# A fused attention and mixture-of-experts kernel: half-row score products on unpadded keys, and another order of gathers and weight splits in the first block of the last layer

## The chip, the cores and the metric

One Trainium2 chip, one of its cores. The metric is the device time of one execution in microseconds (us). The kernel before has a median of 1069.2 us over three runs (1066.33 to 1070.52). All data are float32 in the reference.

## What is computed

Three layers, one after the other, on 2304 tokens (4 sequences of 576) of width 512.

```python
# 1: attention with decay, 8 heads of 64
scores = scale * np.matmul(q, k.transpose(0, 1, 3, 2))
Dmat = np.where(rel >= 0, gamma[:, None, None] ** rel[None, :, :], 0.0)
attn = np.matmul(scores * Dmat[None], v)
# 2: 8 experts, the two best of each token by noisy logits
h = np.maximum(x[mask] @ w1[e], 0.0)                  # 512 -> 1024
out[mask] += top2_w[mask, k, None] * (h @ w2[e])      # 1024 -> 512
# 3: one dense layer of width 2048
h = x @ w_in
g = h * np.cos(h)
return g @ w_out
```

## The kernel before

**Layout of the time.** The program is written for one core with a manual order: each engine runs its instructions in the order in which the Python code emits them. Four stages follow one another in the span: attention with gating and routing (0 to about 165 us), expert 0's second part and experts 1 to 7 (to 639 us), the first block of the last layer (to 689 us), and eight more blocks of the last layer.

**Attention.** There are 20 tiles, five a sequence: four of 128 tokens (`c < 4`) and a tail of 64 (`c == 4`). The loop over `j` runs from -2 to 20. In iteration `j` it issues the loads of tile `j + 4` on SyncE's queue (SP: `load_tile`, L329 queries, L335 keys, L343 keys and values by rows), scales the queries of tile `j + 2` (`decay`, L419, on GpSimd from tile 4 on), makes the score products of tile `j + 1` (`scores`), the gate products of `j - 1` (`gate`, L501) and the outputs of `j` (`outputs`: L469 state, L474 scores times values, L488 the new state), and stores the rows of `j - 1` (L514, SP again). Eight heads lie as four pairs `hp`: partitions 0 to 63 hold one head of a pair, 64 to 127 the other (`s`).

The keys of a full tile lie in a tile `kb` with zeros beside them: for half `s`, only the 64 partitions of that half hold keys, the others hold zeros that were set once at the start (L318, L319). So each score product (L445) runs over all 128 rows although half of them are zeros:

```python
kb[64 s : 64 s + 64, hp, s, :] = keys          # two loads of 512-byte pieces a tile, L335
matmul(p[:, i, s, :], KT[j][:, hp, s, :], QT[j][:, hp, :])    # L445, 8 a tile, 2 passes each
```

The product is masked by VectorE from PSUM (L446), two instructions of 128x512 a tile. PSUM tiles named `ph` come from three buffers. The tail tile has its own form (L455).

**The planner.** Routing (top-2, ranks, tables) is a generator of VectorE instructions that `pump()` puts between the attention's own. `spent(pe, dve)` adds planned TensorE and VectorE time; `pump` emits routing steps as long as the planned VectorE time is less than the planned TensorE time plus a slack. The scores count 0.87 us of TensorE a half. After the attention, the first half of expert 0 (`layer1(0, 0)`, `layer2(0, 0)`) is TensorE work beside the last routing steps.

**Zeros.** `ZERO` gives, for each of seven stores of 1 MB of zeros to the end of `ys` (`zero_overflow`, L373, SP's queue), the iteration at which it is issued; 20 and more count steps behind the attention loop.

**Last layer.** A block is two tiles of 128 tokens; there are nine. `mlp1(i, parts)` makes eight products (L1192, 24 matmuls of 128x256 each), and for each of them `h cos h`: ScalarE L1197 and L1203, VectorE L1198, L1199, L1200, L1204; then the result is split in a high part (ScalarE, L1209) and a low part `gl` (L1210). `mlp2` multiplies by the second weights (L1222, 96 matmuls of 128x512). The rows of block `i + 1` are fetched by `fetch` (L1152, 16 indirect gathers on GpSimd) and combined and transposed by `turn2` (ScalarE L1170 and L747, VectorE L1171, L755 and L748), which writes `x2h` and `x2l`, the operands of `mlp1(i + 1)`.

In block 0 eight weight units are still to be split into high (ScalarE, L289) and low part (L290) by `split_unit`. `SP0` gives the steps of `mlp1` after which one is split, `SPP` those of them whose low part is GpSimd's (0, 3, 6, 9, of which three are used); the others are VectorE's. `FS0 = 1` gather is emitted a step of block 0, the rest behind `mlp1`. `GLP0 = 4`: `gl` of the first four products is GpSimd's in block 0, that of the last four VectorE's; in later blocks all are GpSimd's (`GLP = 8`).

Of the kernel before, what the change touches and what calls it, by code (L numbers as in the profile page):

```python
# [10 lines left out]
F32 = mybir.dt.float32  # L11
# [14 lines left out]
NC = 5  # L26
# [19 lines left out]
ZERO = (11, 13, 22, 27, 27, 29, 33)  # L46
# [3 lines left out]
GLP = 8  # L50
GLP0 = 4
FS = 1
FS0 = 1
SPP = (0, 3, 6, 9)
SP0 = (0, 1, 2, 3, 4, 5, 6, 7, 8, 9)
# [159 lines left out]
def moe_kernel(ctx, tc, x, out, dbg=None, phases="ABC"):  # L215
# [99 lines left out]
    for i in range(LOOK):  # L315
        t = ca.tile([128, HP, 2, 128], F32, name=f"kb{i}")
        eng = nc.gpsimd if i else nc.vector
        eng.memset(t[:64, :, 1, :], 0.0)  # L318
        eng.memset(t[64:, :, 0, :], 0.0)  # L319
        KB.append(t)  # L320
# [10 lines left out]
    def load_k(j):  # L331
        b, c = divmod(j, NC)
        kb, src = (KB[(4 * b + c) % LOOK], x["kt"][4 * b + c]) if c < 4 else (KBT, x["ktt"][b])
        for s in range(2):
            nc.sync.dma_start(kb[s * 64:(s + 1) * 64, :, s, :],  # L335
                              src[s * 64:(s + 1) * 64].rearrange("p (a t) -> p a t", a=HP))
        KT[j] = kb
# [98 lines left out]
    def scores(j):  # L436
        b, c = divmod(j, NC)
        am = wk.tile([128, HP, 2, 128], F32, name="am", bufs=2)
        if c < 4:
            for h2 in range(2):  # L440
                p = ps.tile([128, 2, 2, 128], F32, name="ph", bufs=PHB)
                for i in range(2):
                    hp = 2 * h2 + i
                    for s in range(2):
                        nc.tensor.matmul(p[:, i, s, :], KT[j][:, hp, s, :], QT[j][:, hp, :], start=True, stop=True)  # L445
                nc.vector.tensor_tensor(  # L446
                    am[:, 2 * h2:2 * h2 + 2].rearrange("p a s q -> p (a s) q"),
                    p.rearrange("p a s q -> p (a s) q"),
                    bs["mask"][:, None, :].to_broadcast([128, 4, 128]), op=OP.mult)
                AM[j] = am  # L450
                yield
# [445 lines left out]
    for j in range(-2, NTILE + 1):  # L897
# [12 lines left out]
        if 0 <= j + 1 < NTILE:  # L910
            decay_v(j + 1)
            for _ in scores(j + 1):
                spent(0.87, 0.6)
                pump()
# [261 lines left out]
    def mlp1(i, parts):  # L1176
# [7 lines left out]
        for s in range(10):  # L1184
# [20 lines left out]
            if 0 <= s - 2 < 8:  # L1205
# [4 lines left out]
                (nc.gpsimd if g < (GLP if i else GLP0) else nc.vector).tensor_tensor(  # L1210
# [91 lines left out]
    for i in range(len(blocks)):  # L1302
# [3 lines left out]
        for _ in mlp1(i, parts):  # L1306
            if n in SP0 and state["split"] < len(units):
                split_unit(nc.gpsimd if n in SPP else nc.vector)
            steps(fg, FS if i else FS0)
            n += 1  # L1310
        while state["split"] < len(units):
            split_unit()
        drain(fg)
        drain(turn2(i + 1))
# [23 lines left out]
```

## Time and profile before

| | us |
|---|---|
| median of three runs | 1069.2 (1066.33 to 1070.52) |
| profiled execution | 1059.2 |
| its span, first to last instruction | 1057.3 |
| TensorE busy, mean granted clock | 995.3, 0.966 |
| VectorE, GpSimd, ScalarE busy | 688.6, 445.8, 370.1 |

TensorE's share is 94%, so what counts is where TensorE is not busy, and where it is busy with more or slower work than needed. The share is an average over stages that differ: in the attention the DMA engines are nearly as full as TensorE, in the last layer they are nearly idle.

### The profile page before, as it was taken

The page shows a single profiled execution, that of the slowest core. Times are in us where ns is not written, and L with a number is a line of the kernel's source. Part 1 is how long each engine was busy: PE and PEld are TensorE (multiplying, and loading weights), DVE is VectorE, ACT ScalarE, POOL GpSimd, SP SyncE. Part 2 cuts the span into 40 slices and gives each one's busy share as a digit, 9 for nine tenths or more (in the row PEclk, how much of TensorE's full clock was granted, in tenths as well). Part 3 has the DMA queues.
Part 4 walks back from the last instruction along what each step waited for, and adds up shares of the span by engine and source line. Part 5 has one row for each costly group of instructions (what it writes and reads, how often), then busy time and mean ns, then how long its engine had stood idle before and what let it go on. Part 6 is the DMA issues. An engine that isn't in the chain of part 4 may idle for free.

```text
span 1057.3 us, 17808 instructions
## 1 busy us (share of the span) xinstructions
PE 995.3 (94%) x6845; PEld 928.5 (88%) x6845; DVE 688.6 (65%) x1364; ACT 370.1 (35%) x657; POOL 445.8 (42%) x439
## 2 busy tenths in 40 slices
PE   8989986879899999999899989999999999999998
PEld 7778875869898989989899989798988989899897
DVE  4688971638587676858586447865848567484662
ACT  2422410323141323323142334543535445353451
POOL 6343436351506142341500064736547474564711
PEclk9999988869999999999999999989999999999999
DMA  9898494336576565657563544211010110101110
GB/s 277 270 261 266 120 295 121 100 101 182 157 209 185 180 204 164 215 147 238 160 209 102 141 138 135 73 33 48 21 46 23 43 35 32 50 18 46 30 24 20
DMA packets 85846, 135.37 MB, mean 128 GB/s; under 512 B 13376, under 2 KB 51648, under 8 KB 85760
## 3 DMA queue, kind: packets, MB, share of 16 engines
q1 hardware_dynamic: 76048, 113.74, 36.2%
q0 software_dynamic: 9568, 20.20, 7.3%
q8 instruction: 55, 0.90, 0.4%
q10 hardware_dynamic: 144, 0.27, 0.1%
q14 instruction: 31, 0.25, 0.1%
HBM read 106.25 MB, written 35.26 MB: 134 GB/s over the span
## 4 chain that ended last, share of the span: by engine, by line
PE 84%; DMA 5%; issue 4%; DVE 4%; SPq 1%; ACT 1%; POOL 0%; ACTq 0%; DVEq 0%; POOLq 0%
PE py L1222 18%; PE ph L818 14%; PE ph L797 10%; PE ph L1192 9%; PE pt L797 8%; PE pt L1192 5%; DMA qr<-qt 4%; PE ptab L797 4%; PE ptab L818 3%; PE pt L818 3%; PE ptab L1192 3%; PE ph L445 1%; PE py L818 1%; PE py L469 1%; PE py L474 1%
## 5 line engine op out<-in xcount | busy, mean ns | idle before, releaser
L722 POOL DMA_INDIRECT rows<-xs,gidx x140 | 139.1, 993 | 227.9 <-DVE xt L755 186.7
L1152 POOL DMA_INDIRECT y<-ys,slot x144 | 139.9, 972 | 56.3 <-issue 26.5
L1210 POOL TENSOR_TENSOR gl<-t,gh 128x512 fp32r<-128x512 f32 x68 | 88.6, 1303 | 140.8 <-issue 111.1
L818 PE MATMUL ph<-hh,hb 128*128 128x360 f32 (+2 forms) x312 | 98.8, 317 | 4.9 <-issue 4.6
L818 PE MATMUL ph<-hh,lb 128*128 128x360 f32 (+2 forms) x312 | 98.9, 317 | 4.2 <-issue 4.1
L818 PE MATMUL ph<-hl,hb 128*128 128x360 f32 (+2 forms) x312 | 98.9, 317 | 2.5 <-issue 2.5
L1200 DVE TENSOR_SCALAR t<-t 128x512 int32<-128x512 int32 x72 | 72.8, 1011 | 2.5
L1171 DVE SCALAR_TENSOR_TENSOR y<-y,wts,y 128x128 f32<-128x128 f32 x72 | 34.4, 510 | 59.1 <-DMA y<-ys,slot 52.1
L1198 DVE TENSOR_SCALAR t<-t 128x512 f32<-128x512 f32 x72 | 37.4, 519 | 51.0 <-ACT t L1197 51.0
L747 ACT ACTIVATE xh<-xt 128x512 fp32r<-128x512 f32 (+1 forms) x35 | 21.6, 617 | 137.7 <-DVE xt L755 118.7
L818 PEld LDWEIGHTS ph<-hh,lb 128*128 128x128 f32 x312 | 60.9, 195 | 6.8 <-issue 6.7
L818 PEld LDWEIGHTS ph<-hh,hb 128*128 128x128 f32 x312 | 61.4, 197 | 5.1 <-issue 5.1
L818 PEld LDWEIGHTS ph<-hl,hb 128*128 128x128 f32 x312 | 60.8, 195 | 4.3 <-issue 4.3
L1203 ACT ACTIVATE t<-t,cbias 128x512 f32<-128x512 f32 x72 | 51.9, 722 | 32.9 <-DVE t L1200 32.1
L802 ACT ACTIVATE hh<-pt 128x256 fp32r<-128x256 f32 (+2 forms) x48 | 20.0, 416 | 110.0 <-PE pt L797 77.2
L1222 PE MATMUL py<-hd,gl 128*128 128x512 f32 (+1 forms) x152 | 57.7, 380 | 0.8 <-DVE gl L1210 0.8
L1222 PE MATMUL py<-hb,gl 128*128 128x512 f32 (+1 forms) x152 | 58.4, 384 | 0.0
L1222 PE MATMUL py<-lb,gh 128*128 128x512 f32 (+1 forms) x152 | 58.4, 384 | 0.0
L1222 PE MATMUL py<-hb,gh 128*128 128x512 f32 (+1 forms) x152 | 58.3, 384 | 0.0
L290 POOL TENSOR_TENSOR lb<-st,hb 128x1024 fp32r<-128x1024 f32 x7 | 16.9, 2423 | 97.4 <-PE ptab L797 58.1
L797 PE MATMUL ph<-xh,ha 128*128 128x360 f32 (+3 forms) x236 | 47.7, 321 | 10.5 <-issue 6.1
L797 PE MATMUL ph<-xl,ha 128*128 128x360 f32 (+3 forms) x236 | 49.0, 322 | 9.2 <-issue 9.0
(307 smaller groups left out, 2747.2 us busy)
## 6 DMA issues: line engine op xcount, KB each, us to landing
st<-w SPq DMA_DIRECT2D x64, 512.0 KB
kv<-kv SPq DMA_DIRECT2D x16, 512.0 KB
ci<-wi SPq DMA_DIRECT2D x16, 512.0 KB
wc<-cy SPq DMA_DIRECT2D x32, 256.0 KB
ci<-wo SPq DMA_DIRECT2D x16, 512.0 KB
st<-wc SPq DMA_DIRECT2D x16, 512.0 KB
ys<-c_zero SPq DMA_DIRECT2D x7, 1024.0 KB
qr<-qt SPq DMA_DIRECT2D x20, 256.0 KB
```

The lines of the kernel that those rows point to most:

```text
L722: nc.gpsimd.indirect_dma_start(out=t[:, g, :], out_offset=None, in_=xs.rearrange("n (a d) -> (n a) d", a=4), in_offset=bass.IndirectOffset ...
L747: nc.scalar.activation(hi, src, AF.Copy)
L797: nc.tensor.matmul(p[:, :n], w[a][:, dc, (f % 2) * 128:(f % 2 + 1) * 128], XE[e, g][b][:, dc, :n], start=(i == 0), stop=(i == 3 * DC - 1))
L818: nc.tensor.matmul(p[:, :n], w[a][:, f % 2, c * 128:(c + 1) * 128], HE[e, g][b][:, f, :n], start=(i == 0), stop=(i == 3 * FC - 1))
L1152: nc.gpsimd.indirect_dma_start(out=t[:, g, :], out_offset=None, in_=(ys if i else ys[:FIRST]).rearrange("n (a d) -> (n a) d", a=4), in_off ...
L1171: nc.vector.scalar_tensor_tensor(y0[:, g], y1[:, g], w1, y0[:, g], op0=OP.mult, op1=OP.add)
L1192: nc.tensor.matmul(p[:, f, :], w[a][:, dc, f * 128:(f + 1) * 128], X2[i][b][:, dc, :], start=(k == 0), stop=(k == 3 * DC - 1))
L1198: nc.vector.tensor_scalar(t, t, -MAGIC, None, op0=OP.add)
L1200: nc.vector.tensor_scalar(t.bitcast(I32), t.bitcast(I32), 0x7FFFFFFF, None, op0=OP.bitwise_and)
L1203: nc.scalar.activation(t, t, AF.Sin, scale=-1.0, bias=cbias[:, 1:2])
L1210: (nc.gpsimd if g < (GLP if i else GLP0) else nc.vector).tensor_tensor(fl(gl), T[g], fl(gh.bitcast(F32)), op=OP.subtract)
L1222: nc.tensor.matmul(ps_[tb][:, :c1 - c0], parts[f // 2][b][:, f % 2, tb * 128:(tb + 1) * 128], w[a][:, f % 2, c0:c1], start=(f + k == 0), s ...
```

## The change

In the attention, the zeros beside the keys go. `kb` holds 128 partitions of keys, loaded by one transfer of 2 KB pieces, and each score product runs over the 64 rows of its half, the products of the two halves taking turns and writing two PSUM tiles. The planner counts 0.5 us a half in place of 0.87. Two of the seven zero stores, issued at iterations 11 and 13, move to steps 18 and 24 behind the attention loop.

In block 0 of the last layer, the gathers of block 1 are emitted four a step, so all 16 in the first four steps. No split is GpSimd's in the loop of `mlp1`: six are VectorE's (after steps 0, 1, 3, 5, 7, 9), the last two are GpSimd's behind the loop, each followed by one step of `turn2(1)`. `gl` is VectorE's for products 0 to 4 and GpSimd's for 5 to 7.

```diff
 PHB = 3
 STB = 3
 QPOOL = 4
-ZERO = (11, 13, 22, 27, 27, 29, 33)
+ZERO = (22, 27, 27, 29, 33, 38, 44)
 LOOK = 4
 WJ = 3
 T0_AT = ()
-GLP = 8
-GLP0 = 4
 FS = 1
-FS0 = 1
-SPP = (0, 3, 6, 9)
-SP0 = (0, 1, 2, 3, 4, 5, 6, 7, 8, 9)
+FS0 = 4
+SP0 = (0, 1, 3, 5, 7, 9)
 
 CG_1 = (6, 8, 9, 11, 13, 15)
 CG_2 = (1, 2, 3, 4, 5)
@@
     dq = [dq0[:, :HP * 128]] + [ca.tile([128, HP * 128], F32, name=f"dq{c}") for c in range(1, NC)]
     KB = []
     for i in range(LOOK):
-        t = ca.tile([128, HP, 2, 128], F32, name=f"kb{i}")
-        eng = nc.gpsimd if i else nc.vector
-        eng.memset(t[:64, :, 1, :], 0.0)
-        eng.memset(t[64:, :, 0, :], 0.0)
+        t = ca.tile([128, HP, 128], F32, name=f"kb{i}")
         KB.append(t)
     KBT = ca.tile([128, HP, 2, TAIL], F32, name="kbt")
     SB = [ca.tile([128, HP, 128], F32, name=f"sb{i}") for i in range(2)]
@@
 
     def load_k(j):
         b, c = divmod(j, NC)
-        kb, src = (KB[(4 * b + c) % LOOK], x["kt"][4 * b + c]) if c < 4 else (KBT, x["ktt"][b])
+        if c < 4:
+            KT[j] = KB[(4 * b + c) % LOOK]
+            nc.sync.dma_start(KT[j].rearrange("p a t -> p (a t)"), x["kt"][4 * b + c])
+            return
         for s in range(2):
-            nc.sync.dma_start(kb[s * 64:(s + 1) * 64, :, s, :],
-                              src[s * 64:(s + 1) * 64].rearrange("p (a t) -> p a t", a=HP))
-        KT[j] = kb
+            nc.sync.dma_start(KBT[s * 64:(s + 1) * 64, :, s, :],
+                              x["ktt"][b][s * 64:(s + 1) * 64].rearrange("p (a t) -> p a t", a=HP))
+        KT[j] = KBT
 
     def load_kv(j):
         b, c = divmod(j, NC)
@@
         b, c = divmod(j, NC)
         am = wk.tile([128, HP, 2, 128], F32, name="am", bufs=2)
         if c < 4:
-            for h2 in range(2):
-                p = ps.tile([128, 2, 2, 128], F32, name="ph", bufs=PHB)
-                for i in range(2):
-                    hp = 2 * h2 + i
-                    for s in range(2):
-                        nc.tensor.matmul(p[:, i, s, :], KT[j][:, hp, s, :], QT[j][:, hp, :], start=True, stop=True)
-                nc.vector.tensor_tensor(
-                    am[:, 2 * h2:2 * h2 + 2].rearrange("p a s q -> p (a s) q"),
-                    p.rearrange("p a s q -> p (a s) q"),
-                    bs["mask"][:, None, :].to_broadcast([128, 4, 128]), op=OP.mult)
+
+            pp = [ps.tile([128, HP, 128], F32, name="ph", bufs=PHB) for _ in range(2)]
+            for hp in range(HP):
+                for s in range(2):
+                    h = slice(s * 64, s * 64 + 64)
+                    nc.tensor.matmul(pp[s][:, hp, :], KT[j][h, hp, :], QT[j][h, hp, :], start=True, stop=True)
+            for s in range(2):
+                nc.vector.tensor_tensor(am[:, :, s, :], pp[s], bs["mask"][:, None, :].to_broadcast([128, HP, 128]),
+                                        op=OP.mult)
                 AM[j] = am
                 yield
         else:
@@
         if 0 <= j + 1 < NTILE:
             decay_v(j + 1)
             for _ in scores(j + 1):
-                spent(0.87, 0.6)
+                spent(0.87 if (j + 1) % NC == NC - 1 else 0.5, 0.6)
                 pump()
         if j >= -1:
             next(late, None)
@@
                 gh = cw.tile([128, 2, 256], F32R, name=f"gh{g}")
                 gl = cw.tile([128, 2, 256], F32R, name=f"gl{g}")
                 nc.scalar.activation(fl(gh), T[g], AF.Copy)
-                (nc.gpsimd if g < (GLP if i else GLP0) else nc.vector).tensor_tensor(
+                (nc.gpsimd if i or g > 4 else nc.vector).tensor_tensor(
                     fl(gl), T[g], fl(gh.bitcast(F32)), op=OP.subtract)
                 parts.append((gh, gl))
             yield
@@
         fg = fetch(i + 1)
         for _ in mlp1(i, parts):
             if n in SP0 and state["split"] < len(units):
-                split_unit(nc.gpsimd if n in SPP else nc.vector)
+                split_unit()
             steps(fg, FS if i else FS0)
             n += 1
+        drain(fg)
+        tg = turn2(i + 1)
         while state["split"] < len(units):
-            split_unit()
-        drain(fg)
-        drain(turn2(i + 1))
+            split_unit(nc.gpsimd)
+            steps(tg, 1)
+        drain(tg)
         if i + 1 < len(blocks):
             mlp2(i, (0, 1), parts)
         else:
```

## Rows read from the trace of the kernel before

**Rows 1.** The page: busy time of each engine.

```profile
PE 995.3 (94%) x6845; PEld 928.5 (88%) x6845; DVE 688.6 (65%) x1364; ACT 370.1 (35%) x657; POOL 445.8 (42%) x439
```

**Rows 2.** By stretch: us, busy us (instructions) of PE, PEld, DVE, ACT, POOL; clock, DMA share, GB/s.

```profile
14.40:115.50 101.10, 91.97 (x916) 80.03 (x917) 77.38 (x233) 30.24 (x71) 45.65 (x49) 0.97 0.91 264
...
140.00:152.00 12.00, 11.83 (x77) 11.20 (x77) 8.55 (x37) 2.91 (x6) 2.42 (x1) 0.89 1.05 357
...
105.70:130.00 24.30, 22.39 (x205) 19.75 (x202) 22.41 (x85) 10.18 (x23) 10.28 (x10) 0.93 0.50 130
```

**Rows 3.** The chain that ended last, attention: start, us, what (x passes).

```profile
16.65 0.35 PE pt L501 x8
17.00 1.09 PE py L469 x8
...
20.31 1.79 PE ph L445 x16
...
25.77 0.89 PE ph L455 x8
...
98.31 8.40 DMA qr<-qt
```

**Rows 4.** SyncE's queue: the key loads (ns min/median/max), then two zero stores.

```profile
L335 SPq DMA_DIRECT2D kb<-kt x32: 539/545/911, 1.2 to 100.1; - x32
...
84.77 0.62 SPq L373 DMA_DIRECT2D ys<-c_zero  x1
...
97.62 0.59 SPq L373 DMA_DIRECT2D ys<-c_zero  x1
```

**Rows 5.** The gathered rows: ns min/median/max, first and last start.

```profile
L764 PE MATMUL pt<-ident,rows x8: 271/272/273, 164.3 to 165.1; 128*128 128x128 f32 x8
...
L727 POOL DMA_INDIRECT rows<-xs,gidx x3: 949/949/991, 154.6 to 157.1; - x3
```

**Rows 6.** Busy time by stretch, blocks 1 and 2 of the last layer.

```profile
689.40:737.50 48.10, 48.09 (x290) 44.00 (x291) 29.48 (x45) 20.39 (x36) 25.72 (x24) 0.94 0.12 34
737.50:782.60 45.10, 45.10 (x290) 41.01 (x289) 28.87 (x44) 20.27 (x36) 25.70 (x24) 1.00 0.13 36
```

**Rows 7.** Engines in order of time, block 0: start, us, what [idle before].

```profile
638.92 0.63 PE L1192 MATMUL pt<-x2h,hc 128*128 128x256 f32 x4
...
689.40 1.22 PE L1192 MATMUL ptab<-x2h,hc 128*128 128x256 f32 x4 [3.95 <-issue]
...
645.73 0.69 ACT L1197 ACTIVATE t<-pt,cbias 128x512 f32<-128x512 f32 x1 [7.86 <-DMA ys<-y]
...
647.45 2.40 POOL L290 TENSOR_TENSOR lb<-st,hb 128x1024 fp32r<-128x1024 f32 x1 [18.27 <-ACT hb L289]
...
647.71 2.42 DVE L1200 TENSOR_SCALAR t<-t 128x512 int32<-128x512 int32 x1
...
651.30 0.44 DVE L1200 TENSOR_SCALAR t<-t 128x512 int32<-128x512 int32 x1
...
671.22 2.10 DVE L1200 TENSOR_SCALAR t<-t 128x512 int32<-128x512 int32 x1
...
680.42 1.14 DVE L1171 SCALAR_TENSOR_TENSOR y<-y,wts,y 128x128 f32<-128x128 f32 x4
```

**Rows 8.** Busy time by stretch, gather bursts and slow stretches of TensorE.

```profile
388.40:395.80 7.40, 5.55 (x20) 3.93 (x19) 3.36 (x7) 0.00 (x0) 4.58 (x5) 0.77 0.50 154
...
625.60:631.50 5.90, 2.40 (x11) 1.48 (x10) 2.38 (x7) 0.41 (x1) 2.84 (x3) 0.93 0.17 44
...
378.60:394.30 15.70, 14.13 (x92) 12.71 (x90) 9.41 (x16) 2.75 (x4) 12.07 (x12) 0.92 0.63 191
397.80:408.00 10.20, 10.20 (x68) 10.20 (x67) 4.93 (x11) 0.96 (x2) 7.91 (x8) 1.00 0.45 133
607.80:629.30 21.50, 19.84 (x117) 18.98 (x116) 7.86 (x13) 6.82 (x13) 16.76 (x16) 1.00 0.54 167
...
646.00:662.00 16.00, 16.00 (x136) 16.00 (x135) 14.98 (x18) 10.62 (x16) 11.68 (x8) 1.00 0.45 144
```

## The prediction

> **What bounds the kernel now.** I read the busy times first: TensorE has 94% of the span [rows 1], so a saving must be TensorE idle time or needless TensorE work, in the stage that has it. Then the busy time by stretch and the chain of waits, stage by stage. In the attention loop, from the scores of tile 2 to those of tile 19 (101.1 us, 17 tiles), TensorE is busy 92.0 us, the DMA engines 0.91 of the time, VectorE 77.4 us [rows 2]. Two resources are nearly full together, and the chain there alternates between TensorE and query loads, such as one of 8.40 us [rows 3]. In the last layer the DMA engines are at 0.13 and a block takes 45.1 us, all of it TensorE [rows 6]; only blocks 0 and 1 take longer.
>
> **The change, part by part.**
>
> *Score products.* A full tile's 16 passes take 1.79 us, 0.112 us each [rows 3]. With half rows there are as many passes with as many columns; what can be won is that the passes of the two halves run side by side. No row has a half-row product. Bounds: 0.90 us a tile if the halves overlap fully, 1.79 us if they take turns. Eight passes on a fourth of the columns take 0.35 us, 0.044 each, but their weights are narrower too [rows 3]; that says that array parts can work in parallel, not that full-width loads can. To this comes a change of form: the eight full-array passes right behind the column-split gate products take 1.09 us, where eight that follow full-array passes take 0.89 [rows 3]. So one change costs 0.2 us, and the change adds one a tile, since the scores now follow full-array work in another form. I take 0.9 + 0.2 = 1.1 us, nearer to the parallel row, so 0.7 us less for each of the 14 full tiles in the loop: 9.8 us of TensorE work.
>
> The Trainium skill disagrees with itself here. "TensorE: Matmul & The Clock Gate", LDWEIGHTS, has a weight load cost its columns whatever its rows are: estimated from that page's 1.2 GHz, 107 ns, near the 0.112 us of the row, and the halves would take turns. "TensorEngine Tiling (Array Packing)", Key Properties, lets tiles load weights and multiply in parallel. By the first a tile stays at 1.79 us, by the second at about 0.9. No run here shows which.
>
> *Masks.* Still two 128x512 VectorE instructions a tile. But both products end together, so the first mask starts some half a product later; two of three `ph` buffers are taken at once. The routing steps around them cover it; if not, 0.4 us a tile.
>
> *Key loads.* One issue of 0.545 us in place of two, 16 times [rows 4]; SP's loads and row stores behind it move up, worth at most that much at the start. Bytes stay, pieces grow from 512 bytes to 2 KB. The rows bound this: a stretch mostly of 512-byte row stores moves 130 GB/s at share 0.50 (260 when full), one mostly of 2 KB zeros 357 at 1.05 (340) [rows 2]. For 3.7 MB of keys in the loop that is 14.1 against 10.8 us, so 0 to 3.3; I take 2, since the first stretch has other small pieces. The memsets at the start lie beside the first load: nothing.
>
> *Zeros.* Two stores of 1 MB, at 84.77 and 97.62 on SP's queue right ahead of query loads [rows 4], leave the loop. At 357 GB/s each is 2.9 us of full DMA time [rows 2]: 5.9.
>
> *The loop's sum.* DMA: 0.91 x 101.1 = 92.0, less 5.9 and 2, is 84. TensorE: 92.0 less 9.8 is 82. VectorE stays at 77. If the fullest is again used to 0.91, the loop takes 84 / 0.91 = 92 us: 9 us less. Bounds: 0, if TensorE is still at 92 and loses nothing but cover; 14, at 0.97 use.
>
> *What it hands on.* The planner counts less TensorE time in the loop, so it puts fewer routing steps there; they come later, on VectorE, which then waits less on data but has the same work in a shorter time. And the two zero stores come behind five others, where the DMA engines are full already [rows 2]: up to 5.9 us later for what is behind them. The three row gathers are issued to 158.1 us and read by TensorE at 164.3 [rows 5], so most of that is covered. Price 0 to 6; I take 1. Attention in all: 8 us.
>
> *Block 0.* It starts on TensorE at 638.92 and block 1 at 689.40 [rows 7]: 50.5 us, 5.4 more than a block. Block 1 starts behind an idle stretch at a mean clock of 0.94 and takes 48.1 instead of 45.1 [rows 6]: 3.0 more. These 8.4 us are all there is. Their cause is `turn2(1)`: VectorE starts it at 680.42 [rows 7], and then waits for gathers. GpSimd's splits and `gl` make VectorE slow: L1200 takes 2.42 us beside a split and 0.44 without [rows 7]. Six of L1198 and L1200 are stretched so, from 647.71 to 671.22 [rows 7], 7.7 us in all. The change frees VectorE of these and gives it one split (1.2 us) and one `gl` (0.6) more, so `turn2(1)` starts 5.9 us earlier, at 674.5. Even if it took the same 9 us as now, the operands are there by 683.5, where TensorE without idle time ends the block (638.92 + 45.1 = 684.0). The two last splits on GpSimd, some 2.4 us each behind three `gl`, end just ahead of their use; a miss there is under 1 us.
>
> *The gathers.* The first can go once the `ys` stores have landed; ScalarE waits for these until 645.73 [rows 7]. Then 16 follow on GpSimd, with no work between them, at 1.3 us each (16 in 21.5 us [rows 8]): to about 666. Where gathers follow one another so long, TensorE slows with no wait that the profile names: 12 gathers from 378.6 on, and from 388.4 to 395.8 only 20 matmuls pass in 7.4 us, where 68 passed in 10.2 us of the next, shorter burst of eight [rows 8]. That is a loss of 7.4 - 20 x 0.15 = 4.4 us. The 16 gathers ahead of block 0 do it at 625.6, 17.8 us after their start: 11 in 5.9 us, 4.2 lost [rows 8]. `mlp1(0)` now runs 136 matmuls in 16 us beside scattered gathers [rows 8]. A burst there would slow it from 656 (10 us in) or 664 (18 us in) until some 2 us after the last gather, 668. At 0.39 us a matmul instead of 0.12 the loss is 8.4 or 2.8 us; middle 5.6, and 0.4 for the clock, which was at 0.77 in such a stretch [rows 8]. No reason in the rows makes this a gain. Block 0 in all: 8.4 - 6 = 2.4; I count 2.
>
> "Runtime: NRT & Kernel Launch", Instruction fetch mechanics, in the Trainium skill holds that refilling an engine's instructions costs mostly nothing. If the slowing is a late refill, which the rows do not tell, the measurement decides against that; by the page block 0 would gain all 8.4 us.
>
> **Sum.** 8 + 2 = 10 us. The profiled execution has 1059.2 us (span 1057.3 and 1.9 around it), so its like would have 1049.2. The median of the runs is 10.0 higher, 1069.2, and I move the sum onto it: 1059.2, say 1059. A measurement of this kernel tells 0.5%, 5.3 us, from no change.
>
> **Rivals.**
>
> *No slowing by the burst* (0.18): 8 + 8.4 = 16, 1053. For it: the burst of eight slows nothing, that of 16 only 17.8 us in [rows 8]. Against: `mlp1(0)` has shorter matmuls than the stretch that stood those 17.8 us. This is also what the Runtime page would have.
>
> *The halves take turns* (0.24): TensorE keeps its 92 us and gets 0.2 x 14 = 2.8 more for the change of form. Of its 9.1 us of idle time in the loop, mostly waits for queries, some 4.5 go with the lighter DMA load. 4.5 - 2.8 - 1 + 2.4 = 3: 1066. For it: 0.112 us a pass is longer than what 128 columns should stream in (256 columns pass in 0.118 [rows 8]), so weight loads bound the scores now. This is the first of the two pages' case.
>
> *Slower: weight loads that no longer hide* (0.10). If loading one half cannot go beside a product of the other, each of the 16 passes shows load and stream one behind the other: 0.112 + 0.06, 1.0 us a tile, 14 us on TensorE, which is then alone the bound. 14 - 4.5 (idle time that it fills) + 1 - 2.4 = 8 slower: 1077. It decides once a pass costs over some 0.15 us.
>
> *The routing becomes the bound* is inside the forecast's own range: VectorE, at 77 us of 92, would let the later routing steps cost 5 of the 6 us above instead of 1, and the attention gives 4.
>
> **How the numbers follow.** Forecast 0.45, 1053 to 1064; then 1053, 1066 and 1077 with 0.18, 0.24 and 0.10; 0.03 is left. Range 1048 to 1069: up to the best with both gains at 12 and 8.4 (1069.2 - 20.4), down to the halves taking turns with no DMA gain. Faster: 0.38 of the forecast, 0.18, and 0.07 of the rest, 0.63. Slower 0.10. Same 0.27.
>
> **What would show it.** Right: 16 score passes in 0.9 to 1.2 us; the loop from tile 2 to tile 19 at some 92 us; block 1 of the last layer 45 us long, with no idle time ahead of it; a slow stretch of TensorE at 656 to 668 (less what the attention saved). Wrong: scores at 1.8 us; the attention's gain gone where `gidx` or the gathers come late; block 0 longer than 50.5 us, which makes the burst dearer than what it buys.

## The result and the profile after

| | before, us | changed, us |
|---|---|---|
| median, nine runs each | 1069.2 (1065.3 to 1073.6) | 1061.8 (1055.9 to 1063.4) |
| ratio of the runs, 95% interval | | 0.9919 (0.9893 to 0.9945) |
| profiled execution, its span | 1059.2, 1057.3 | 1055.9, 1054.0 |
| mean granted clock of TensorE | 0.966 | 0.958 |

By the ratio the change is 8.7 us faster, 0.8%: more than the 0.5% that a measurement of this kernel can tell. 1059 (1048 to 1069) was forecast. The two profiled executions differ by 3.3 us only, since that of before lies 10.0 below its median and that of the changed kernel 5.9; so the pair shows where time moved, and the sums below are checked against the medians.

Line numbers of the changed kernel are a few lower: scores L442 (L445 before), state L465 (L469), expert layers L793 and L814, gathers L718 and L1148, `mlp1` L1188, `mlp2` L1218, splits L286 and L287.

The page of the changed kernel, the busy times that answer to [rows 1]:

```profile
PE 990.4 (94%) x6845; PEld 919.1 (87%) x6845; DVE 683.8 (65%) x1364; ACT 370.6 (35%) x657; POOL 441.4 (42%) x431
```

Its chain that ended last, in the attention, which answers to [rows 3]:

```profile
35.95 1.09 PE ph L442 x16
37.04 0.35 PE pt L497 x8
37.40 1.09 PE py L465 x8
```

A tile's 16 score passes take 1.09 us; they took 1.79. The eight state products behind them stay at 1.09.

Its busy time by stretch (columns as in [rows 2]): the loop from tile 2 to tile 19; a whole expert; two slow stretches, one in expert 0 and one in a later expert; block 0; the slow stretch in it; block 1.

```profile
14.00:100.10 86.10, 79.77 (x916) 66.51 (x916) 72.52 (x214) 30.59 (x71) 42.99 (x45) 0.98 0.85 269
...
275.80:337.10 61.30, 58.96 (x387) 57.20 (x386) 43.16 (x80) 17.37 (x29) 20.50 (x21) 0.94 0.62 177
...
160.00:179.70 19.70, 6.58 (x21) 4.59 (x19) 1.97 (x7) 0.42 (x1) 12.29 (x13) 0.57 0.19 50
...
377.70:385.30 7.60, 4.78 (x15) 3.00 (x13) 1.99 (x4) 0.63 (x1) 5.23 (x5) 0.74 0.54 168
...
634.50:689.10 54.60, 50.47 (x292) 44.20 (x291) 38.14 (x60) 26.76 (x44) 28.51 (x23) 0.94 0.34 94
...
657.60:666.10 8.50, 4.97 (x18) 3.85 (x18) 3.96 (x7) 2.56 (x4) 5.01 (x5) 0.72 0.42 129
...
689.10:734.20 45.10, 45.10 (x290) 41.01 (x290) 28.62 (x44) 19.79 (x35) 25.72 (x24) 1.00 0.13 36
```

The loop takes 86.1 us in place of 101.1 [rows 2], with the same 916 matmuls and 12.2 us less of busy TensorE. Block 0 takes 54.6 in place of 50.5 [rows 7]; block 1 is down from 48.1 to a plain block's 45.1 [rows 6]. In the row at 160 us, 21 matmuls run in 19.7 us beside 13 gathers.

Engines in order of time in the changed kernel (start, us, what, idle time before): the first matmul of expert 0's second part; the first gather of block 0; what ScalarE, VectorE and GpSimd do later in block 0, to be held beside [rows 7].

```profile
152.13 0.78 PE L793 MATMUL pt<-xh,ha 128*128 128x296 f32 x4 [1.07 <-DVE xl L744]
...
642.02 0.95 POOL L1148 DMA_INDIRECT y<-ys,slot  x1 [17.46 <-DMA ys<-y]
...
665.59 0.69 ACT L1193 ACTIVATE t<-pt,cbias 128x512 f32<-128x512 f32 x1 [5.95 <-PE pt L1188]
...
667.57 0.43 DVE L1196 TENSOR_SCALAR t<-t 128x512 int32<-128x512 int32 x1
...
676.35 3.27 DVE L1167 SCALAR_TENSOR_TENSOR y<-y,wts,y 128x128 f32<-128x128 f32 x4
```

The same first matmul of expert 0's second part in the kernel before:

```profile
167.00 0.78 PE L797 MATMUL pt<-xh,ha 128*128 128x296 f32 x4 [1.19 <-ACT xh L747]
```

It stood 14.9 us later. But block 0 begins at 634.5, where it began at 638.9. Of the 14.9 us, 10.5 are gone by the end of the experts, in code that the change does not touch. In block 0 VectorE's steps are no longer stretched (0.43 us); instead ScalarE waits 5.95 us for TensorE, in the middle of the slow stretch.

So there were three questions: what the attention is worth, and by which of its edits; whether the experts really take some of it back; and whether the gathers make the slow stretches.

### The profile page after: what moved, and what is told of

The parts are those of the page before. It is cut to its first block, busy times and chain, and to the rows that moved or that the text cites. A ratio compares the mean times of both kernels' runs of the same rounds, so it can differ in the third digit from the quotient of the medians.

```text
span 1054.0 us, 17779 instructions
## 1 busy us (share of the span) xinstructions
PE 990.4 (94%) x6845; PEld 919.1 (87%) x6845; DVE 683.8 (65%) x1364; ACT 370.6 (35%) x657; POOL 441.4 (42%) x431
## 4 chain that ended last, share of the span: by engine, by line
PE 86%; issue 5%; DVE 4%; DMA 3%; SPq 1%; ACT 0%; DVEq 0%; ACTq 0%
PE py L1218 19%; PE ph L814 14%; PE ph L793 10%; PE ph L1188 10%; PE pt L793 8%; PE pt L1188 7%; PE ptab L814 4%; PE ptab L793 4%; PE pt L814 3%; PE ptab L1188 3%; PE py L814 1%; DMA st<-w 1%; DMA kv<-kv 1%; PE ph L442 1%; DVE sb L643 1%
## 5 line engine op out<-in xcount | busy, mean ns | idle before, releaser
L718 POOL DMA_INDIRECT rows<-xs,gidx x140 | 138.6, 990 | 236.3 <-DVE xt L751 194.1
L1148 POOL DMA_INDIRECT y<-ys,slot x144 | 141.1, 980 | 73.5 <-DMA ys<-y 38.9
L814 PE MATMUL ph<-hh,lb 128*128 128x360 f32 (+2 forms) x312 | 100.7, 323 | 3.0 <-issue 3.0
L814 PE MATMUL ph<-hh,hb 128*128 128x360 f32 (+2 forms) x312 | 100.2, 321 | 3.1 <-issue 2.9
L814 PE MATMUL ph<-hl,hb 128*128 128x360 f32 (+2 forms) x312 | 100.1, 321 | 0.4 <-issue 0.4
L1167 DVE SCALAR_TENSOR_TENSOR y<-y,wts,y 128x128 f32<-128x128 f32 x72 | 38.5, 570 | 55.8 <-DMA y<-ys,slot 47.4
L1194 DVE TENSOR_SCALAR t<-t 128x512 f32<-128x512 f32 x72 | 35.1, 487 | 55.9 <-ACT t L1193 55.9
L1196 DVE TENSOR_SCALAR t<-t 128x512 int32<-128x512 int32 x72 | 67.0, 930 | 2.5
L814 PEld LDWEIGHTS ph<-hh,lb 128*128 128x128 f32 x312 | 61.9, 199 | 6.1 <-issue 6.1
L814 PEld LDWEIGHTS ph<-hh,hb 128*128 128x128 f32 x312 | 62.5, 200 | 4.9 <-issue 4.9
L814 PEld LDWEIGHTS ph<-hl,hb 128*128 128x128 f32 x312 | 62.2, 199 | 1.7 <-issue 1.7
L1199 ACT ACTIVATE t<-t,cbias 128x512 f32<-128x512 f32 x72 | 51.9, 721 | 24.8 <-DVE t L1196 23.8
L1218 PE MATMUL py<-hb,gh 128*128 128x512 f32 (+1 forms) x152 | 59.0, 388 | 0.2 <-issue 0.2
L1218 PE MATMUL py<-lb,gh 128*128 128x512 f32 (+1 forms) x152 | 58.9, 387 | 0.0
L1218 PE MATMUL py<-hb,gl 128*128 128x512 f32 (+1 forms) x152 | 58.8, 387 | 0.0
L793 PE MATMUL ph<-xh,ha 128*128 128x360 f32 (+3 forms) x236 | 48.1, 323 | 10.6 <-issue 6.1
L1218 PE MATMUL py<-hd,gl 128*128 128x512 f32 (+1 forms) x152 | 57.5, 378 | 0.0
L1218 PE MATMUL py<-ld,gh 128*128 128x512 f32 (+1 forms) x152 | 57.5, 378 | 0.0
L1218 PE MATMUL py<-hd,gh 128*128 128x512 f32 (+1 forms) x152 | 57.5, 378 | 0.0
L793 PE MATMUL ph<-xl,ha 128*128 128x360 f32 (+3 forms) x236 | 47.6, 319 | 9.6 <-issue 9.6
```

The lines of the kernel that those rows point to most:

```text
L718: nc.gpsimd.indirect_dma_start(out=t[:, g, :], out_offset=None, in_=xs.rearrange("n (a d) -> (n a) d", a=4), in_offset=bass.IndirectOffset ...
L793: nc.tensor.matmul(p[:, :n], w[a][:, dc, (f % 2) * 128:(f % 2 + 1) * 128], XE[e, g][b][:, dc, :n], start=(i == 0), stop=(i == 3 * DC - 1))
L814: nc.tensor.matmul(p[:, :n], w[a][:, f % 2, c * 128:(c + 1) * 128], HE[e, g][b][:, f, :n], start=(i == 0), stop=(i == 3 * FC - 1))
L1148: nc.gpsimd.indirect_dma_start(out=t[:, g, :], out_offset=None, in_=(ys if i else ys[:FIRST]).rearrange("n (a d) -> (n a) d", a=4), in_off ...
L1167: nc.vector.scalar_tensor_tensor(y0[:, g], y1[:, g], w1, y0[:, g], op0=OP.mult, op1=OP.add)
L1194: nc.vector.tensor_scalar(t, t, -MAGIC, None, op0=OP.add)
```

## The experiments

Each experiment is named by its label. They ran on different chips, and that turned out to be the main thing to know: on the chip of the first comparison, and on that of e11_old_zeros, e4_zeros and e12_spread_again, the kernel before takes 1069 us; on the chips of the other experiments it takes 995. Each ratio is against the kernel before on the same chip.

### The halves of the change

**e1_attention**: the changed kernel with the block 0 part put back; beside these constants, the lines for `gl`, the splits and `turn2` as before.

```
-FS0 = 4
-SP0 = (0, 1, 3, 5, 7, 9)
+GLP = 8
+GLP0 = 4
+FS0 = 1
+SPP = (0, 3, 6, 9)
+SP0 = (0, 1, 2, 3, 4, 5, 6, 7, 8, 9)
```

> The changed kernel with its block 0 put back as before (one gather a step, splits and gl shared between VectorE and GpSimd as before). Theory: the attention edits give the whole gain and the block 0 part gives nothing or costs 1 us. Then this kernel is 8 to 12 us faster than the one before, level with the changed kernel or 1 us ahead of it; block 0 takes 50.5 us again, with no slow stretch of TensorE in it, and block 1 takes 48.1. Rival: what the attention gains is mostly lost again in the experts, and the difference of the medians comes from blocks 0 and 1. Then this kernel is 5 us faster at most.

Measured: 983.8 against 995.2, ratio 0.9886 (0.9867 to 0.9904), 11.4 us faster. Its busy time by stretch: the loop, one expert, block 0, block 1.

```profile
13.90:102.70 88.80, 82.14 (x916) 68.76 (x916) 69.50 (x214) 30.55 (x71) 42.03 (x44) 0.94 0.83 261
...
291.50:346.10 54.60, 54.60 (x385) 54.60 (x385) 42.42 (x78) 17.52 (x29) 20.25 (x21) 1.00 0.71 212
564.50:615.40 50.90, 45.75 (x290) 40.72 (x288) 40.03 (x59) 26.58 (x44) 30.57 (x25) 1.00 0.33 100
615.40:662.10 46.70, 46.70 (x288) 42.65 (x289) 29.77 (x45) 20.65 (x37) 25.68 (x24) 0.96 0.11 35
```

The attention is most of the change, as the theory had it. The expert's row was not expected: 54.6 us with TensorE busy throughout at full clock (2.4 GHz), where the changed kernel took 61.3. On this chip no expert has a slow stretch.

**e2_block0**: the kernel before with the block 0 part alone (the same lines, the other way round).

> The kernel before with the block 0 part of the change alone (16 gathers first on GpSimd, six splits on VectorE, the last two on GpSimd). Theory: the burst of gathers slows TensorE for some 8.5 us in block 0, which takes 54 us in place of 50.5, and block 1 gets 3 us back: 1 us slower, 0 to 3. Rival of the theory: the longer block 0 of the changed kernel was chance, and the 8.4 us of blocks 0 and 1 come back: 4 to 8 us faster.

Measured: 991.2, ratio 0.9961 (0.9946 to 0.9976), 3.9 us faster: the lower end of the rival's case. Blocks 0 and 1 together take 95.4 us (573.0 to 668.4); in e1_attention, with the old order, 97.6. Its busy time by stretch, `mlp1(0)` and `mlp2(0)`:

```profile
573.00:596.00 23.00, 22.99 (x191) 22.99 (x192) 16.80 (x30) 12.03 (x18) 11.63 (x11) 1.00 0.46 134
596.00:623.00 27.00, 24.44 (x100) 18.94 (x99) 22.06 (x32) 15.69 (x27) 17.04 (x13) 0.95 0.23 75
```

In the first, TensorE is busy all the time beside the burst: nothing slows it on this chip. The second takes 27.0 us, where a plain block has 22.1 left for it (45.1 less the 23.0 of `mlp1`). What is late there is shown by e9_splits_first below.

**e3_scores**: the kernel before with the scores, the keys and the planner's 0.5 alone; that is e1_attention with the zero stores at their old places.

```
-ZERO = (22, 27, 27, 29, 33, 38, 44)
+ZERO = (11, 13, 22, 27, 27, 29, 33)
```

> The kernel before with half-row score products, unpadded keys and the planner's 0.5 alone; the zero stores stay where they were and block 0 is as before. Theory: the scores carry about two thirds of the attention's gain, so the scores of tile 19 start at some 105 us (115.5 before, 100.1 in the changed kernel) and the kernel is 6 to 8 us faster. Rival: the two zero stores taken from the loop are what counted, as its DMA load was 0.91: tile 19 at 110 or later, and 3 us faster at most.

Measured: 979.8, ratio 0.9849 (0.9829 to 0.9869), 15.0 us faster by the ratio, twice the theory's 6 to 8, with tile 19's scores at 102.1. Scores, keys and planner alone give at least as much as all the attention edits together. Its loop:

```profile
12.20:102.10 89.90, 81.58 (x916) 68.08 (x916) 75.59 (x216) 30.39 (x71) 44.45 (x46) 0.96 0.88 288
```

With the two zero stores in it the loop is about as long as in e1_attention (88.8): the DMA engines did not set its length. The shortest loop of all, in e10_spread_and_splits below, has the two stores in it too:

```profile
14.30:97.40 83.10, 79.36 (x915) 66.38 (x915) 70.22 (x214) 30.54 (x71) 41.33 (x44) 0.98 0.92 300
```

### The zeros

**e11_old_zeros**: the changed kernel with the `ZERO` line above. **e4_zeros**: the kernel before with the new places. Both ran where the kernel before takes 1069.

> The changed kernel with the zero stores where the kernel before has them (two of the seven between the query loads of the loop). Theory from the pair of earlier runs that differ in this alone (979.8 with the old places, 983.8 with the new): in the changed loop VectorE is the fullest (41.6 of 45 us), the DMA engines are at 0.70 and have room for two stores of 1 MB, while the new places put seven of them ahead of the gathers; so the old places are 2 to 4 us faster than the changed kernel, a ratio of 0.982 where the kernel before takes 995. Rival, as the prediction had it: taking them from the loop gives the attention several us, so the old places are 3 us slower or more: 0.989.

> The kernel before with the new places of the zero stores alone. Theory: with full-row scores the loop's DMA load is 0.91 of its time, so leaving out two stores of 2.9 us there wins up to 6 us, of which their place ahead of the gathers takes back as much: within 2 us of the kernel before. Rival: the new places cost in any loop: 3 us slower.

Measured: e11_old_zeros 1061.5, ratio 0.9944 (0.9927 to 0.9960); the changed kernel has 0.9919 (0.9893 to 0.9945), and the intervals overlap. e4_zeros 1070.8, ratio 1.0016 (0.9994 to 1.0038). So on this chip the new places are worth nothing that can be told, in either loop. The 4 us by which the old places were ahead (e3_scores against e1_attention) are not seen here; where the kernel before takes 995 no second pair differs in the zeros alone, so whether the new places cost something there stays open. The loop of e4_zeros:

```profile
15.10:114.00 98.90, 90.70 (x914) 79.05 (x914) 74.80 (x230) 29.87 (x70) 43.62 (x48) 0.97 0.88 248
```

It is 2.2 us shorter than the loop before [rows 2], not 5.9, and expert 0's second part then begins at 168.3, no earlier than the 167.0 of before.

### The changed kernel once more, and its halves side by side

**e8_changed_again**: the changed kernel, unaltered, on a chip where the kernel before takes 995.

> The changed kernel itself, unaltered, beside the kernel before on the chip of this call. The four runs ahead of it were on a chip where the kernel before takes 995 us and TensorE has no slow stretch beside the experts' gathers. Theory: the change is worth about 15 us where the gathers slow nothing (11.4 for the attention edits and 3.9 for block 0, as the two halves gave there), and 9 where they do, because there the experts take some of it back. So a ratio of 0.985 if the kernel before is again at 995, 0.992 if it is at 1069. Rival: the 8.6 us of the first comparison are the worth of the change on any chip, and the two halves overlap: 0.991 on both.

Measured: 981.4 against 995.1, ratio 0.9858 (0.9843 to 0.9872), 14.1 us faster. The theory's 0.985 is inside the interval, the rival's 0.991 is not. Its busy time by stretch: the loop, a burst of 20 gathers, block 0, an expert.

```profile
15.00:104.80 89.80, 81.33 (x915) 67.93 (x915) 74.64 (x214) 30.51 (x71) 40.73 (x44) 0.96 0.81 255
...
271.00:296.30 25.30, 25.30 (x178) 25.30 (x177) 18.21 (x38) 4.58 (x8) 19.04 (x20) 1.00 0.62 184
...
567.30:616.10 48.80, 46.23 (x289) 40.98 (x290) 38.40 (x61) 27.40 (x44) 28.65 (x23) 1.00 0.34 103
293.90:348.50 54.60, 54.60 (x386) 54.60 (x385) 42.40 (x78) 17.53 (x29) 20.24 (x21) 1.00 0.72 212
```

Twenty gathers follow one another in 25.3 us, and TensorE is busy in all of them. What slows TensorE on one chip does nothing to it on another.

**e6_halves_grouped**: the changed kernel, with the passes of one half first.

```
-            for hp in range(HP):
-                for s in range(2):
+            for s in range(2):
+                for hp in range(HP):
```

> The changed kernel with the 16 score passes of a tile in another order: the eight of the upper half of the rows first, then the eight of the lower half, instead of one of each in turn. Theory: a pass takes 0.068 us in place of 0.112 because the two halves of the array work side by side; grouped by half they cannot, a tile's scores take some 1.8 us again, and the kernel is 5 to 10 us slower than the changed one. Rival: a pass on 64 rows is short by itself; the tile stays at 1.1 us and the time is the changed kernel's within 2 us.

Measured: 984.3, ratio 0.9877 (0.9857 to 0.9898), 2.9 us slower by the medians than e8_changed_again beside it and 1.9 by the ratios, whose intervals overlap: under the theory's 5 to 10, and the times alone do not decide against the rival. The chain does; first that of e8_changed_again, then that of this kernel:

```profile
94.53 1.09 PE ph L442 x16
...
99.91 1.09 PE ph L442 x16
```

```profile
99.48 1.64 PE ph L442 x16
...
105.41 1.64 PE ph L442 x16
```

The same 16 passes on the same rows and columns take 1.64 us when the passes of a half follow one another, and 1.09 when the halves alternate. How they do it shows in the start of one tile's scores, cut off some 0.37 us after its first pass: in the changed kernel, in e6_halves_grouped and in the kernel before.

```profile
35.88 0.60 PE L442 MATMUL ph<-qt,kb 64*128 64x128 f32 x6
```

```profile
43.01 0.60 PE L442 MATMUL ph<-qt,kb 64*128 64x128 f32 x3
```

```profile
34.62 0.60 PE L445 MATMUL ph<-qt,kb 128*128 128x128 f32 x3
```

Six passes have started where the halves alternate, three in the other two. In the first, the passes start in pairs, one of either half 0.007 us apart, and the pairs 0.112 us apart. A half-row pass that follows one of its own half starts 0.112 us after it, just as a full-row pass does. So half rows by themselves gain nothing, and the whole gain is the other half running beside: eight pairs at 0.112 us and 0.2 us of a change of form are the 1.09. The grouped kernel is below 1.79 only because three passes of the second half run beside the last ones of the first.

By 0.55 us for each of 14 tiles the loop should be 7.7 us longer than that of e8_changed_again. It is 6.9 longer (14.2 to 110.9, 96.7 us): TensorE's work sets its length. Of these, 4.8 us are left where expert 0's second part begins (162.3 against 157.5), and the two profiled executions differ by 4.7.

### The gathers

**e7_spread_experts** and, the same kernel where the kernel before takes 1069, **e12_spread_again**: in experts 1 to 6 four gathers behind each of five steps of the first layer.

```
+PACE = (1, 4, 8, 12, 16)
...
             for _ in layer1(e, g):
                 n += 1
+                if paced and n in PACE:
+                    nc.gpsimd.tensor_copy(tick, HE[e, g][0][0:1, (n - 1) % FC, 0:1].bitcast(F32))
+                    gather(e + 1, PACE.index(n))
```

> The changed kernel, where in experts 1 to 6 the 20 row gathers for the next expert no longer go one behind the other: four are issued after each of the steps 1, 4, 8, 12 and 16 of the first layer, each group behind a copy of one element of that step's output on GpSimd. Expert 0's gathers and the last layer stay as they are. Theory: TensorE's stretches without a named wait come from 12 and more gathers in a row. The six from 201 us on (16.6, 7.5, 6.5, 7.7, 6.9 and 8.4 us, in which 90 matmuls pass that need some 0.15 us each) vanish, 40 us; without the first, which may have another cause, 26. So 1022 to 1036, while the stretch at 160 to 180 us stays. Rival: the stretches lie where they do because of the code that TensorE runs there (a refill of its instructions), and the gathers only coincide: no change within 3 us, the stretches stay.

Measured: 976.2, ratio 0.9806 (0.9790 to 0.9821). On that chip there were no stretches to take away, so the run decides nothing between the two cases; an expert still gained 0.7 us over e1_attention's:

```profile
293.30:347.20 53.90, 53.90 (x385) 53.90 (x385) 42.48 (x78) 17.52 (x29) 22.95 (x25) 1.00 0.69 214
```

> The changed kernel with the experts' gathers spread, as in the earlier run of the same, beside the changed kernel's relatives on the chip of this call. Theory: on a chip where a burst of 20 gathers shows no slow stretch of TensorE it wins 0.6 us an expert, 3.6 us: 0.981. On a chip that shows them it wins 25 to 40 us: below 0.97. Rival on such a chip: the slow stretches stay where they are with the gathers spread, and it wins 4 us at most.

Measured: 1028.8 against 1068.8, ratio 0.9623 (0.9602 to 0.9644): 40 us faster than before, and 33 faster than e11_old_zeros (1061.5) on the same chip and than the changed kernel's 1061.8 of the first comparison. Its busy time by stretch: expert 0's burst, which was left in a row; two of the stretches that remain in later experts; the one in block 0, left too; an expert.

```profile
161.30:181.60 20.30, 5.65 (x19) 4.01 (x18) 1.49 (x8) 0.42 (x1) 12.69 (x14) 0.61 0.28 85
...
272.90:276.40 3.50, 2.36 (x11) 1.30 (x9) 0.06 (x1) 0.00 (x0) 1.89 (x2) 1.00 0.68 194
386.80:390.60 3.80, 2.23 (x12) 1.23 (x10) 0.42 (x1) 0.38 (x1) 1.89 (x2) 1.00 0.65 190
...
629.90:638.80 8.90, 4.91 (x18) 3.64 (x17) 4.47 (x8) 2.22 (x4) 5.27 (x6) 0.69 0.40 140
318.10:376.00 57.90, 56.56 (x386) 55.74 (x385) 42.01 (x78) 17.31 (x29) 24.35 (x25) 0.97 0.66 200
```

Inside one execution the stretches shrink where the gathers were spread (3.5 and 3.8 us, where the changed kernel's row has 7.6) and stay where they were not (20.3 and 8.9, against 19.7 and 8.5). That is the theory's case and not the rival's. What is left comes at the end of eight gathers that still stand in a row.

### Block 0's last splits

**e9_splits_first**: both last splits ahead of `turn2(1)`.

```
         while state["split"] < len(units):
             split_unit(nc.gpsimd)
-            steps(tg, 1)
         drain(tg)
```

> The changed kernel with one thing altered in block 0: both last splits go to GpSimd ahead of the two steps of turn2(1), where the second split stood behind the first step. Theory: of the 5 us that block 0 still takes over a plain block, the last split has most: its copy on ScalarE waits behind turn2's work, it ends on GpSimd at 609.4 in the run with spread gathers, TensorE waits 1.9 us for it and does the next eight matmuls in 0.43 us each in place of 0.23. Ahead of turn2 it ends some 3 us before its use: 3.5 us faster than the changed kernel beside it. Rival: turn2(1) then comes later by the split's time and TensorE waits for it at the start of block 1: within 1 us of the changed kernel.

What it was aimed at, in e8_changed_again beside it: TensorE's waits from 540 to 670 us (total, times, longest), and then the second split and its reader in order of time.

```profile
PE py L1218 <- POOL ld L287: 1.9, 1, 1.9
PE py L1218 <- DVE ld L287: 0.6, 1, 0.6
PE pt L1188 <- ACT x2h L743: 0.2, 1, 0.2
```

```profile
611.01 2.35 POOL L287 TENSOR_TENSOR ld<-st,hd 128x1024 fp32r<-128x1024 f32 x1 [3.38 <-ACT hd L286]
...
613.42 0.50 PE L1218 MATMUL py<-ld,gh 128*128 128x512 f32 x1 [1.93 <-POOL ld L287]
```

The same waits in e9_splits_first:

```profile
PE ptab L1188 <- ACT x2h L743: 1.7, 1, 1.7
PE py L1218 <- DVE ld L287: 0.3, 1, 0.3
```

Measured: 979.2 (975.5 to 986.5), ratio 0.9852 (0.9827 to 0.9878), against e8_changed_again's 0.9858: no difference that can be told. The wait for the split is gone, and one of 1.7 us for `x2h`, `turn2`'s product, has taken its place. In e8_changed_again the matmuls behind the wait ran at full clock again, unlike in the run that the expectation was taken from, so only the waits themselves were to be had. Blocks 0 and 1 take 92.9 us (560.8 to 653.7) in place of 93.9. The rival's mechanism did most of it.

### Two sums of parts

**e10_spread_and_splits**: e7_spread_experts with the edit of e9_splits_first and the old `ZERO`.

> The changed kernel with three things altered: the experts' gathers spread as in the run before (four behind each of five steps), both last splits ahead of turn2(1), and the zero stores where the kernel before has them. Theory on a chip without slow stretches: 4 us for the spread gathers (an expert took 54.0 us in place of 54.6), 3.5 for the splits, 0 to 4 for the zeros, so 8 to 11 us faster than the changed kernel beside it. On a chip with slow stretches 25 to 40 us more, as six stretches of 6.5 to 16.6 us go. Rival: the spread gathers come later and turn() waits for them, and the experts take 55 us or more: no faster than the kernel with the splits alone.

Measured: 973.0, ratio 0.9780 (0.9767 to 0.9792), 8.4 us faster than e8_changed_again beside it and 22 faster than the kernel before. It is the fastest of all where the kernel before takes 995; where that takes 1069 it was not run, and e12_spread_again is the fastest.

**e13_all_spread**: expert 0's gathers and block 0's broken up as well, with the edit of e9_splits_first; its main lines:

```
+F0_AT = {0: 4, 1: 4, 8: 8}
+G_AT = (1, 6, 11, 16)
+G_AT0 = (1, 4, 7)
...
+                if e + 1 < E and n in (G_AT if e else G_AT0):
+                    behind(e, (G_AT if e else G_AT0).index(n), HE[e, g][0][0:1, (n - 1) % FC, 0:1])
...
+            steps(fg, FS if i else F0_AT.get(n, 0))
```

> The changed kernel with every long burst but one broken up: the experts' gathers four at a time behind every fifth step of the first layer (the last four in the second layer), expert 0's four at a time behind its steps 1, 4, 7 and two turned blocks, and in block 0 eight gathers at the start and eight after step 8, behind two gl; both last splits ahead of turn2(1). Only the 16 gathers ahead of block 0 stay in a row. Theory: on the chip with slow stretches the one of 20.3 us in expert 0 (16 matmuls pass) goes, 18 us, the five of 3.5 to 4.3 that eight in a row leave, 2 to 2.5 us each, and that of 8.9 in block 0 with its clock, 7 us, and 2 us come from the splits: 990 to 1003 where the spread of the experts alone gave 1028.8 (the kernel before at 1069). On a chip without them only the splits and the even experts count: 968 to 975 (before at 995). Rival: a limit on instructions that come in beside gathers in all, not in a row: the stretches split into more and shorter ones, and the time stays above 1015 on the first chip.

Measured, where the kernel before takes 995: 985.7, ratio 0.9925 (0.9900 to 0.9950), 11 us above the range and slower than the changed kernel. TensorE's waits from 540 to 630 us:

```profile
PE py L1220 <- POOL ld L289: 8.9, 1, 8.9
PE py L1220 <- DVE ld L289: 0.3, 1, 0.3
```

The second eight gathers of block 0 stood on GpSimd ahead of the last `gl` and the splits, which ended 8.9 us too late. Most experts took 54.0 us, as spread elsewhere; block 0 took 56.3 and lost more than the experts had won. With slow stretches this kernel was not run, so whether expert 0's 20 us can be had stays open.

## Why the prediction was right or wrong

**The time** came out right, 1059 against 1061.8, with two errors of opposite sign in it: that it came so near is in part luck.

*Score products: right.* 1.1 us a tile was forecast and 1.09 came, with both of its terms: 0.9 for halves side by side and 0.2 for the change of form, as the starts of the passes and e6_halves_grouped show. "The halves take turns" falls, and so does the rival of weight loads that no longer hide: a pass takes 0.068 us in the mean, not over 0.15. The two pages of the Trainium skill that the prediction set against each other do not exclude one another here. "TensorEngine Tiling (Array Packing)", Key Properties, has tiles load weights and multiply in parallel, which the pairs show. By "TensorE: Matmul & The Clock Gate", LDWEIGHTS, a load costs its columns whatever its rows; the trace agrees within one half, where a half-row pass takes the 0.112 us of a full-row one. That the halves then take turns does not follow from it.

*The attention's sum: too small.* 8 us were forecast. Expert 0's second part begins at 163.2, 167.0 and 168.3 in the three traces with the old scores (mean 166.2) and between 149.5 and 158.1 in the ten with the new ones alternating (mean 154.0): 12 us earlier. One pair of executions can show anything from 5 to 19. Kept apart by chip, it is 14 us where the kernel before takes 1069 (two traces with the old scores, three with the new) and 9 where it takes 995 (one and seven), so sums of parts are good to a few us only. The step that failed is the sum of the loop: "if the fullest is again used to 0.91, the loop takes 84 / 0.91 = 92 us". It took the DMA engines for the bound, and so zeros and keys for the source of the gain. Measured, taking the zero stores out gives nothing that can be told (e4_zeros, e11_old_zeros), the loop with them in it, at a DMA share of 0.88 or 0.92, is as short as without, and e6_halves_grouped shows that TensorE's passes set its length. Their term, 9.8 us, was nearly the whole: over all traces loops of 97 to 101 us (mean 99.0) became 83 to 91 (mean 88.2), 10.8 us shorter. What the keys' larger pieces give by themselves was not run.

*Block 0: wrong in sign on the first chip.* A gain of 2 us was counted. There, blocks 0 and 1 take 99.7 us (634.5 to 734.2) against 98.6 before (638.9 to 737.5): a loss of 1. The slow stretch was forecast for 656 to 668 at a price of 6 us; counted from the start of block 0 that is 17 to 29 us. It came at 657.6 to 666.1, 23 to 32 us after that start, and `mlp1(0)`, 634.5 to 665.5, took 31.0 us where e2_block0 has 23.0: the price was 8. (The 0.39 us a matmul in that sum stands in no row; [rows 8] has 0.37 and 0.54, and 0.47 came.) The other step that failed is "the two last splits on GpSimd [...] end just ahead of their use; a miss there is under 1 us". Where no stretch delays TensorE they miss: it waits 1.9 and 0.6 us in e8_changed_again. So of the 8.4 us that "are all there is", the new order wins 2 to 4 even without the stretch (93.9 and 95.4 us for blocks 0 and 1, against e1_attention's 97.6), and loses what the stretch costs beyond that.

*That the experts take some back is not shown.* The first pair of traces suggested that they lose 10.5 us again. From the start of expert 0's second part to block 0 the kernel before took 471.9 us and the changed one 482.4; but e4_zeros, with the old scores, took 489.3, and e11_old_zeros, with the new, 488.5. Where there are no slow stretches it is 409.4 to 409.9 in every kernel whose experts' gathers were not spread, with the old scores or the new. So the stretches' length varies between executions, and no run shows that the change has a part in it.

*The rival "no slowing by the burst"* (16 us faster) describes the chips where the kernel before takes 995: 14.1 us there. Which case holds differed from chip to chip. The trace of before, with its slow stretches, told it for its own chip only. The Trainium skill's "Runtime: NRT & Kernel Launch", Instruction fetch mechanics, has a refill of instructions mostly hidden. e8_changed_again agrees, with no stretch beside 20 gathers; the changed kernel on the first chip does not, if the stretches are late refills at all. That was not settled: the runs show that they come from gathers in a row, not by what way.

By parts: 12 from the attention less 1 in block 0 is 11 on the first chip, where 8.7 (5.9 to 11.4, by the interval) was measured; on the other kind 12 and 2 to 4, where 14.1 was.

## What to carry to other kernels

Products that fill half of the array's rows are cheap if passes of the two halves alternate: two of them then take the 0.112 us of one. Grouped by half each takes 0.112 by itself, and most of the gain is lost. When two traces differ in a stage that the change does not touch, look at a third execution before explaining it. Long runs of indirect gathers are better spread between steps that pace them, where there is time: on two chips where the kernel before takes 995 an expert took 0.6 to 0.7 us less by it, and on one where it takes 1069 the kernel took 33 us less; but what is queued behind the gathers on GpSimd must still come in time.

## What the runs showed that was not expected

One and the same kernel takes 995 us on some chips and 1069 on others, and the traces differ beside the gathers: an expert takes 54.6 us with TensorE busy throughout on the first kind, and 61.3 us with TensorE busy for 58.96, at a mean granted clock of 0.94, on the second. Nearly all of the 74 us lies between the start of expert 0's second part and block 0 (409 to 410 us against 472 to 489, with the experts' gathers in a row). The runs do not show whether it is the chip itself or something else of that time. On the second kind long rows of gathers bring a stretch in which few matmuls pass with no wait that the profile names (21 in 19.7 us at the worst; eight in a row still bring one of 3.5 to 4.4 in e12_spread_again). In the worst the mean granted clock is 0.57, mostly the lower level, 1.2 GHz, so the matmuls that pass are slow too; but the clock is not the cause, since in e12_spread_again only 11 pass in 3.5 us at a clock of 1.00.

VectorE's instructions beside a split on GpSimd are stretched, in the two forms seen here: freed of splits, `mlp1`'s step takes 0.43 us, where it took 2.42 [rows 7]; but the four combining instructions of `turn2`, 1.14 us before [rows 7], now lie beside a split and take 3.27. The instruction that meets the split is not slowed evenly: it ends just behind the split, 0.28 or 0.29 us in the three cases of L1200 before, 0.14 or 0.15 in the four of the first combining instruction (changed kernel and e8_changed_again), and the other three combining instructions take 0.34 us each. L1199, which has an input from PSUM, takes 0.69 us beside a split too (at 658.5 before).
